# Sums of silu(h) formed in the output stage, conversions spread anew, and each output sum issued behind its product

## The chip, the cores and the metric

The kernel runs on one core of a Trainium2 chip. The metric is device time in microseconds (us), the median of some runs. A core has a matrix engine (TensorE, PE in the profile), a vector engine (VectorE, DVE), a scalar engine (ScalarE, ACT) and GpSimd (POOL), each with a queue of its own that is worked off in order; DMAs are issued mostly from SyncE's queue (SP). Matmuls read operands from SBUF, the on-chip memory, and add into PSUM, the accumulator memory of eight banks; DVE and ACT read the results there.

## The reference, cut to what matters

```python
def reference(q, k, v, moe_w1, moe_w2, moe_w3, moe_w_out, moe2_w_in, moe2_w_out):
    attn = window_attention(q, k, v)            # 4 x 8 heads x 576 x 64, window of 64
    x = attn.transpose(0, 2, 1, 3).reshape(2304, 512)
    x = ((x @ w1) * (x @ w2)) @ w3 @ w_out      # 512 -> 1024 -> 1024 -> 512
    h = x @ w_in                                # 512 -> 2048
    g = h * (1.0 / (1.0 + np.exp(-h)))          # silu
    return (g @ w_out2).astype(np.float32)      # 2048 -> 512, 2304 tokens
```

The weights arrive as 64-bit floats and are made into 32-bit ones on the chip ("conversion").

## The kernel before, in words

**Arithmetic.** Every product of two 32-bit matrices is three matmul passes: each operand is split into a rounded part (hi, a cast on ACT) and a rest (lo, a subtraction on DVE), and hi·hi, hi·lo and lo·hi are added up in PSUM (`PASSES`). On top of this the last two layers use a Strassen scheme: a 2x2 product of blocks costs seven products k = 0..6 (named A11, A12, A22, S1 to S4 after the left operand) and sums of the operands before and of the results behind.

**Stages.** The attention and the first feed-forward run block by block (`phase_a`, six blocks). During the sixth, `hooks5(n)` interleaves the first preparation for the next layer: slot n counts from 0 to 23 (n5 + n = −24 to −1 in `jobs`). Then comes the **h stage**: 12 pieces of work d (a duo: 256 hidden units by 768 tokens) of seven slots each, `h_slot(d, pos)`, in the order `POS` of the products. A product is 12 matmuls of 128x384. `read` takes its result out of PSUM (ACT or DVE) and applies silu. Then the **output stage**: 36 sets m, nine groups of 256 tokens (`tg`) by four parts of the hidden units (e = m % 4); `out_products(m)` is 7 products of 6 matmuls 128x256, added up over e in two PSUM tiles a and b of two banks each (`AT` says where). After the fourth set of a group `out_sums(tg)` puts the seven results together (one on ACT, then `two`, `u3`, `u4` and the two halves of c on DVE) and stores the group.

**Between the two stages** silu(h) goes through device memory (`gd`). In before `sums_of_g(d - 1, pos)` makes the Strassen sums S1 to S4 of a duo's four blocks while the next duo is computed, two operations of 128x768 on DVE and two on POOL, and `keep` stores seven pieces of 384 KB per duo. The output stage loads seven pieces of a set (`f_load`, two DMAs), casts them (`f_high`: 128x256 and 128x1536 on ACT) and subtracts (`f_low`: the same shapes on DVE), three sets ahead of the products.

**What sets the order.** The source is the order: each engine works off its instructions in the order of the calls below, and waits on semaphores for what it needs. `jobs` is a table from slot to calls: `at(slot, f, ...)`. `convert(n, at, places)` puts the steps of one conversion of w_out2 (loads, ACT L220 and L225, DVE L228 and L232, POOL L237, then sums and stores to `t32`) into slots at−2 to at+7; `PLAN` and the list in `hooks5` say where the eight conversions start. `w_part` (table `W5` for n = 0..3) makes the split operands of w_in out of what `r_load` loads; `o_load` and `o_part` do it for w_out2; `x_raw`, `x_sum`, `x_op` for the tokens. Line L800 is the helper `tt` through which every elementwise sum or difference goes, so its rows are told apart by their tiles: gq, gxb, gxa and gst are the buffers of the h stage, f and xe loaded sets, hi, lo and a their split parts, ot and oc the output sums, ab and a (L707, L709) the first feed-forward's activations.

Of the kernel before, what the change touches and what calls it, by code (L numbers as in the profile page):

```python
# [9 lines left out]
F32 = mybir.dt.float32  # L10
# [12 lines left out]
NB = 384  # L23
# [19 lines left out]
def tile_window_attention_ffn(ctx, tc, qkv, qkp, vp, w1, w2, w3t, w_out, w_in, w_out2, out):  # L43
# [704 lines left out]
    with tc.manual_schedule():  # L748
# [44 lines left out]
        gd = dram.tile([NTG, DUOS, 128, 7, 256], F32, name="gd", tag="gd")  # L793
# [82 lines left out]
        def convert(n, at, places):  # L876
# [5 lines left out]
            (l0, s0, r0, f0, h0, i0, _), (l1, s1, r1, f1, h1, i1, _) = [c.pieces() for c in pair]  # L882
# [23 lines left out]
            for k, f in ((-2, l0), (-1, l1), (0, s0), (0, r0), (1, f0), (1, s1), (2, h0), (2, i0), (2, r1)):  # L906
                jobs.setdefault(at + k, []).append(f)
            for k, f in ((3, f1), (3, h1), (4, i1), (5, sums), (6, more), (6, store_b), (7, store_t)):
                jobs.setdefault(at + k, []).append(f)
# [11 lines left out]
        def o_load(n):  # L921
            t = raw["o", n] = [xe[:, 0:1024], xe[:, 1024:1792]] if n in (1, 3, 5) else [st[2], st[3][:, 0:768]]
            for x, y in zip(t, (slice(0, 4), slice(4, 7))):
                nc.sync.dma_start(out=x, in_=t32[n, :, y].rearrange("p a n -> p (a n)"))

        def o_tiles(n):
# [8 lines left out]
            t = pair_tiles("wo", n - 1, (2, 256))  # L935
            oop[n] = [(x[:, 0], x[:, 1]) for x in t]

        def o_part(n, part):
            if part == 0:
                o_tiles(n)  # L940
            r0, r1 = raw["o", n]
            src = [r0[:, 0:512], r0[:, 512:1024], r1[:, 0:512], r1[:, 512:768]]
# [74 lines left out]
        S2, S3, S1, A22, A12, S4, A11 = range(7)  # L1017

        def read(d, k):
# [9 lines left out]
            elif k == 2:  # L1029
                silu(g["a11", d % 2], h_bank("ha"))  # L1030
            elif k == 3:
                add(nc.vector, one, h_bank("hb"), one)
                add(nc.vector, h_bank("hc"), h_bank("hc"), one)
                silu(g["a12", d % 2], h_bank("hc"))
# [47 lines left out]
        def f_load(m):  # L1082
            if m >= NTG * DUOS:
                return
            if m == 0:
                t = slot("f0", "x0", [6, 256], pool=end), xe[:, 2048:2304]
            elif m == 1 or m % 3 == 0:
                t = xe[:, 0:1536].rearrange("p (a n) -> p a n", a=6), xe[:, 1536:1792]
            elif m == 2 or m % 3 == 1:
                q = slot(f"f{m}", "q", [7, 256])  # L1090
                t = q[:, 0:6], q[:, 6]
            else:
                t = slot(f"f{m}", "xa", [6, 256]), slot(f"fa{m}", "xb", [256])
            raw["f", m] = t
            tg, e = divmod(m, DUOS)
            nc.sync.dma_start(out=t[0], in_=gd[tg, e, :, 0:6])
            nc.sync.dma_start(out=t[1], in_=gd[tg, e, :, 6])

        def f_high(m):
            if m < NTG * DUOS:  # L1100
                n = m % 4
                if n == 3:
                    lo = shared["wo", "p"].rearrange("p a n -> p (a n)")[:, 0:1536].rearrange("p (a n) -> p a n", a=6)
                    a = unit_tile("wo", 6, 3)[:, 512:1024]
# [8 lines left out]
                nc.scalar.copy(out=a[0], in_=raw["f", m][1])  # L1113
                nc.scalar.copy(out=hi, in_=raw["f", m][0])  # L1114

        def f_low(m):
            if m < NTG * DUOS:
                lo, hi, a = sets[m]
                f, fa = raw["f", m]
                sub(nc.vector, a[1], fa, f32(a[0]))  # L1120
                sub(nc.vector, lo, f, f32(hi))

        TERMS = ((A11, 0, 0), (S2, 2, 1), (S3, 0, 1), (S1, 2, 0), (A22, 3, 0), (A12, 1, 0), (S4, 1, 1))
# [3 lines left out]
        def out_products(m):  # L1129
# [5 lines left out]
            for (op, w, half), (x, y, z), first in zip(TERMS, AT, FIRST):  # L1135
                dst = bank[x][:, y, z * 256 : z * 256 + 256]
                for q in range(2):
                    cols = slice(q * 128, q * 128 + 128)
                    lhs = [x[:, cols] for x in a] if op == A11 else [hi[:, op, cols], lo[:, op, cols]]
                    rhs = [x[:, half] for x in oop[2 * e + q][w]]  # L1140
                    for n, (l, r) in enumerate(PASSES):
# [3 lines left out]
                        )  # L1145

        def out_sums(tg):
# [5 lines left out]
            t = slot(f"ot{tg}", "st", [4, 256], bufs=4)  # L1153
            one, u4, two, u3 = [t[:, i] for i in range(4)]
            c = slot(f"oc{tg}", "st", [2, 2, 256], bufs=4)
            nc.scalar.copy(out=one, in_=b[:, 1, 0:256])
            add(nc.vector, two, a[:, 1, 0:256], one)
            add(nc.vector, u3, a[:, 1, 256:512], two)
            add(nc.vector, u4, a[:, 0, 256:512], two)
            halves = [x.rearrange("p (i n) -> p i n", i=2) for x in (a[:, 0], b[:, 0])]  # L1160
            add(nc.vector, c[:, 1], halves[0], t[:, 3:4].to_broadcast([128, 2, 256]))
            j, r = divmod(tg, 3)
            row = j * 2 * NB + r * 128
            nc.sync.dma_start(out=out[row + NB : row + NB + 128, :], in_=c[:, 1].rearrange("p i n -> p (i n)"))
            if tg < NTG - 1:
# [193 lines left out]
```

## Time and profile before

| | |
|---|---|
| three runs | 884.75, 885.05 and 887.29 us, median 885.05 |
| the profiled execution's own time | 887.39 us |
| its span in the trace | 884.9 us |
| PE busy | 827.5 us (94%) |
| DVE, ACT, POOL busy | 650.8, 539.4, 408.2 us |
| end of the sixth block and start of the h stage | 481.6 us |
| start of the output stage's transition | 678.4 us |
| end of the last matmul | 878.9 us |

A row of the table by stretches gives, for each engine, busy time and (x) the number of instructions in a stretch, then the clock that was granted to PE (1.00 is 2.4 GHz, 0.50 is 1.2 GHz), the busy share of the DMA engines and GB/s. A row of the waits gives what an engine stood still for: instruction <- releaser, the sum, how many times, the longest. A row of the timeline gives start, duration, engine, line, what is written and read, and in brackets how long the engine stood idle before it and what ended that. In a grouped row the second number is the mean in ns.

### The profile page before, as it was taken

To read this page: it belongs to the slowest core of one execution; us is meant where nothing else is said; L and a number is where in the kernel's file an instruction comes from. 1 tells how busy PE (TensorE), PEld (TensorE's weight loads), DVE (VectorE), ACT (ScalarE), POOL (GpSimd) and SP (SyncE) were. 2 spreads that over 40 slices of the span, in tenths; PEclk is the share of its full clock that TensorE was granted. 3 is DMA by queue.
4 is the path that set the end of the run, shared out by engine and by line. 5 is a ranking of instruction groups with operands and counts; after the bars stand their busy time and mean duration, and the time that the engine had idled before them with its cause. 6 is when DMAs were issued, how large, how long until landed. Compare 5 with 4: busy or idle time off the path is not lost. (4 is left out here: it accounts for less than half of the span.)

```text
span 884.9 us, 15592 instructions
## 1 busy us (share of the span) xinstructions
PE 827.5 (94%) x5066; PEld 777.4 (88%) x5066; DVE 650.8 (74%) x1419; ACT 539.4 (61%) x1254; POOL 408.2 (46%) x460
## 2 busy tenths in 40 slices
PE   8899999999999999999859999879997969999997
PEld 3455899999999999999859999779897969999997
DVE  8879777788888888883794789968878655545551
ACT  7889778898888998984543345424455344343330
POOL 5767666677676776774672353564232000000000
PEclk9999999999999999999998999998999979999999
DMA  9997235345445445434524567897888687565631
GB/s 309 342 295 236 76 99 164 102 136 183 149 141 172 135 157 168 150 117 143 206 80 149 166 223 254 278 348 242 270 290 303 219 322 264 196 222 198 222 128 38
DMA packets 96689, 174.66 MB, mean 197 GB/s; under 512 B 8160, under 2 KB 64864, under 8 KB 96608
## 3 DMA queue, kind: packets, MB, share of 16 engines
q1 hardware_dynamic: 93008, 168.82, 57.1%
q10 hardware_dynamic: 3600, 4.85, 1.5%
q8 instruction: 40, 0.66, 0.3%
q14 instruction: 41, 0.34, 0.1%
HBM read 119.64 MB, written 54.00 MB: 196 GB/s over the span
## 5 line engine op out<-in xcount | busy, mean ns | idle before, releaser
L693 PE MATMUL ab<-xa,hl 128*128 128x384 f32 x576 | 121.3, 345 | 9.2 <-DVE a L709 6.2
L693 PE MATMUL ab<-xb,hl 128*128 128x384 f32 x570 | 116.7, 337 | 0.0
L693 PEld LDWEIGHTS ab<-xa,hl 128*128 128x128 f32 x576 | 100.3, 191 | 10.7 <-DVE a L709 7.2
L693 PEld LDWEIGHTS ab<-xb,hl 128*128 128x128 f32 x570 | 101.9, 191 | 0.0
L1142 PE MATMUL oa<-wo_w,hi 128*128 128x256 f32 x486 | 89.8, 283 | 0.0
L1142 PEld LDWEIGHTS oa<-wo_w,hi 128*128 128x128 f32 x486 | 75.7, 191 | 0.0
L351 POOL TENSOR_TENSOR klo<-qk,qkhi 64x192 fp32r<-64x192 f32 x110 | 67.3, 612 | 8.4 <-ACT qkhi L345 2.3
L723 PE MATMUL x<-p,wp 128*128 128x384 f32 x360 | 70.4, 344 | 0.0
L474 POOL TENSOR_TENSOR xr<-ot 128x128 f32<-128x128 f32 x55 | 32.7, 595 | 72.9 <-DVE ot L473 56.0
L723 PEld LDWEIGHTS x<-p,wp 128*128 128x128 f32 x360 | 63.3, 192 | 0.0
L237 POOL TENSOR_TENSOR cv_b<-cv_b,cv_r 128x512 int32<-128x512 int32 x32 | 48.6, 1518 | 18.7 <-DVE cv_b L232 10.6
L1114 ACT CAST hi<-f 128x1536 fp32r<-128x1536 f32 x24 | 35.4, 1475 | 35.1 <-PE ob L1142 35.1
L999 PE MATMUL hb<-xop,wi_w 128*128 128x384 f32 x252 | 50.6, 349 | 5.4 <-DVE gxb L800 5.4
L999 PE MATMUL ha<-xop,wi_w 128*128 128x384 f32 x252 | 49.8, 345 | 6.3 <-ACT gq L1008 5.7
L800 DVE TENSOR_TENSOR lo<-f,hi 128x1536 fp32r<-128x1536 f32 x18 | 31.7, 1758 | 30.5 <-ACT hi L1114 30.4
L999 PEld LDWEIGHTS hb<-xop,wi_w 128*128 128x128 f32 x252 | 46.7, 196 | 6.3 <-DVE gxb L800 6.3
L999 PEld LDWEIGHTS ha<-xop,wi_w 128*128 128x128 f32 x252 | 45.1, 191 | 7.5 <-ACT gq L1008 6.1
L999 PE MATMUL hd<-xop,wi_w 128*128 128x384 f32 x252 | 49.1, 341 | 2.3 <-DVE gxb L800 2.2
L1142 PE MATMUL oa<-wo_w,lo 128*128 128x256 f32 x180 | 51.0, 283 | 0.0
L406 ACT ACTIVATE sm<-sm,nm 128x192 f32<-128x192 f32 x110 | 49.3, 449 | 1.4
L999 PEld LDWEIGHTS hd<-xop,wi_w 128*128 128x128 f32 x252 | 44.2, 188 | 4.2 <-DVE gxb L800 3.3
L345 ACT CAST qkhi<-qk 128x768 fp32r<-128x768 f32 x55 | 46.0, 836 | 1.2
(245 smaller groups left out, 2297.5 us busy)
## 6 DMA issues: line engine op xcount, KB each, us to landing
qk<-in_qkv SPq DMA_DIRECT2D x55, 384.0 KB, 3.0
f<-gd SPq DMA_DIRECT2D x24, 768.0 KB, 4.3
gd<-gq SPq DMA_DIRECT2D x24, 384.0 KB, 3.6
gd<-gxb SPq DMA_DIRECT2D x24, 384.0 KB, 3.1
gd<-gst SPq DMA_DIRECT2D x24, 384.0 KB, 2.9
xe<-gd SPq DMA_DIRECT2D x12, 768.0 KB, 4.3
words<-in_w3t SPq DMA_DIRECT2D x16, 512.0 KB, 6.4
words<-in_w SPq DMA_DIRECT2D x16, 512.0 KB, 7.0
```

The lines of the kernel that those rows point to most:

```text
L237: nc.gpsimd.tensor_tensor(out=self.b, in0=self.b, in1=self.r, op=ALU.add)
L345: nc.scalar.copy(out=hi, in_=t)
L351: nc.gpsimd.tensor_tensor(out=k_lo[g % 2][hs, h * 192 : h * 192 + 192], in0=t[hs, n], in1=f32(hi[hs, n]), op=ALU.subtract)
L406: nc.scalar.activation(out=e[:, h, :], in_=x, func=AF.Exp, scale=-1.0, bias=nm[:, h : h + 1], accum_out=sums_of[g % 2][:, h, 0:1])
L474: nc.gpsimd.tensor_tensor(out=xr[:, c, r : r + 128], in0=t[:, 0:128], in1=t[:, 128:256], op=ALU.add)
L693: nc.tensor.matmul(acc, lhsT=w[:, l, fs], rhs=x[k // 2][:, k % 2, r, :], start=(k == 0 and n == 0), stop=(k == 3 and n == 2),)
L723: nc.tensor.matmul(acc, lhsT=wp[f][:, l, o * 128 : (o + 1) * 128], rhs=p[f][:, r, :], start=(f == 0 and n == 0), stop=(f == 7 and n == 2),)
L800: eng.tensor_tensor(out=out, in0=a, in1=b, op=op)
L999: nc.tensor.matmul(bank[name][:, q, 0:NB], lhsT=w[:, l, first + kt], rhs=x[:, kt, r, :], start=(fresh and kt == 0 and n == 0), stop=(kt == ...
L1114: nc.scalar.copy(out=hi, in_=raw["f", m][0])
L1142: nc.tensor.matmul(dst, lhsT=lhs[l], rhs=rhs[r], start=(first and e == 0 and q == 0 and n == 0), stop=(e == DUOS - 1 and q == 1 and n == 2 ...
```

## The change

Five things are changed together.

1. `sums_of_g` is gone. `gd` holds four pieces per duo (A11, A12, A22 and A21), `keep` is called four times, and the sums S1 to S4 are made per set in the output stage, by the new `f_sums(m)`: S1 on POOL (on DVE for sets 0 to 3), S3, S2 and S4 on DVE, 128x256 each. `f_load` is one DMA of 512 KB. Casts and subtractions of a set are 768 + 768 + 256 wide.
2. The buffers of the h stage have new homes: the q buffer is now free during it and takes the loads of the conversions and of some weights; a11 and a12 have one buffer, and nothing is summed in place of a22.
3. The conversions are spread anew: two in the sixth block (at slots 2 and 6), six in the h stage (at 12, 18, 25, 31, 37, 43) instead of three and five; their sign step is one DVE instruction of 512 instead of two of 256.
4. Loads and preparations have new slots (`W5`, `r_load`, `o_load`, `f_load`).
5. `out_sums(tg, op)` is called behind each of the seven products of a group's last set, each time for one sum, instead of once after the set. In the last group the last 128x512 sum is two halves, as before, the first of them behind A12.

```diff
-        S2, S3, S1, A22, A12, S4, A11 = range(7)
...
-                silu(g["a11", d % 2], h_bank("ha"))
+                silu(g["a11"], h_bank("ha"))
...
-        def sums_of_g(d, pos):
-            a11, a12, a22, a21, s2 = g["a11", d % 2], g["a12", d % 2], g["a22"], g["two", d % 2], g["s2"]
-            if pos == 0:
-                keep(d, A12, a12)
-                keep(d, A22, a22)
-            elif pos == 3:
-                add(nc.vector, a22, a21, a22)
-                sub(nc.vector, s2, a22, a11)
-                sub(nc.gpsimd, a11, a21, a11)
-            elif pos == 4:
-                sub(nc.gpsimd, a12, a12, s2)
-                keep(d, S1, a22)
-                keep(d, S2, s2)
-            elif pos == 5:
-                keep(d, S3, a11)
-            elif pos == 6:
-                keep(d, S4, a12)
...
             run_later()
-            if d:
-                sums_of_g(d - 1, pos)
-            if pos == 4:
-                keep(d, A11, g["a11", d % 2])
             run_jobs(7 * d + pos)
+            if pos == 0 and d:
+                keep(d - 1, 1, g["a12"])
+                keep(d - 1, 2, g["a22"])
+            elif pos == 4:
+                keep(d, 0, g["a11"])
+                if d:
+                    keep(d - 1, 3, g["two", 1 - d % 2])
...
+        def f_sums(m, eng=None):
+            if m < NTG * DUOS:
+                f, t = [x.rearrange("p (a n) -> p a n", a=4) for x in raw["f", m]]
+                add(eng or nc.gpsimd, t[:, 0], f[:, 3], f[:, 2])
+                sub(nc.vector, t[:, 1], f[:, 3], f[:, 0])
+                sub(nc.vector, t[:, 2], t[:, 0], f[:, 0])
+                sub(nc.vector, t[:, 3], f[:, 1], t[:, 2])
...
+                if e == DUOS - 1:
+                    out_sums(tg, op)
...
-        W5 = {0: 8, 1: 10, 2: 16, 3: 17}
+        W5 = {0: 8, 1: 15, 2: 17, 3: 19}
...
-                for i, (first, x) in enumerate(((2, 2), (5, 0), (9, 2))):
+                for i, (first, x) in enumerate(((2, 2), (6, 0))):
...
-        PLAN = ((3, 24), (4, 29), (5, 34), (6, 39), (7, 44))
+        PLAN = ((2, 12), (3, 18), (4, 25), (5, 31), (6, 37), (7, 43))
...
         out_products(0)
+        keep(NDUO - 1, 1, g["a12"])
+        keep(NDUO - 1, 2, g["a22"])
+        f_sums(2, nc.vector)
         f_high(2)
         f_low(2)
+        f_load(3)
         product(NDUO - 1, 6)
+        read(NDUO - 1, 6)
+        keep(NDUO - 1, 3, g["two", 1 - NDUO % 2])
         for part in range(4):
             o_part(7, part)
+        f_sums(3, nc.vector)
         f_high(3)
         f_low(3)
-        read(NDUO - 1, 6)
-        for pos in (0, 3, 4, 5, 6):
-            sums_of_g(NDUO - 1, pos)
-        for m in (4, 5, 6):
-            f_load(m)
+        f_load(4)
+        f_load(5)
+        f_load(6)
+        f_sums(4)
         for m in range(1, NTG * DUOS):
+            f_sums(m + 4)
             f_high(m + 3)
             f_low(m + 3)
             f_load(m + 6)
             out_products(m)
-            if m % DUOS == DUOS - 1:
-                out_sums(m // DUOS)
```

The first place is PE's row in the last set of the second group (m = 7). A row is line, operation, out<-in with buffer numbers, the shape, how many alike follow each other, and in brackets the engines whose semaphores it waits for. oa1 and ob1 are the group's PSUM tiles. Before, from the end of the second product (S2) on:

```order
L1142 MATMUL oa1_8152<-wo_w23_7945,wo_p_7946 128x256
L1142 MATMUL oa1_8152<-wo_w17_7795,hi7_8144 128x256 x2
L1142 MATMUL oa1_8152<-wo_w17_7795,wo_p_7946 128x256
L1142 MATMUL oa1_8152<-wo_w21_7943,hi7_8144 128x256 x2
L1142 MATMUL oa1_8152<-wo_w21_7943,wo_p_7946 128x256
L1142 MATMUL oa1_8152<-wo_w19_7797,hi7_8144 128x256 x2
L1142 MATMUL oa1_8152<-wo_w19_7797,wo_p_7946 128x256
L1142 MATMUL oa1_8152<-wo_w23_7945,hi7_8144 128x256 x2
L1142 MATMUL oa1_8152<-wo_w23_7945,wo_p_7946 128x256
L1142 MATMUL oa1_8152<-wo_w20_7774,hi7_8144 128x256 x2
L1142 MATMUL oa1_8152<-wo_w20_7774,wo_p_7946 128x256
L1142 MATMUL oa1_8152<-wo_p_7946,hi7_8144 128x256 x2
```

and with the change, from the same point on:

```order
L1150 MATMUL oa1_8097<-wo_p_7875,lo7_8086 128x256
L1150 MATMUL oa1_8097<-wo_w17_7712,hi7_8087 128x256 [waits DVE_49]
L1150 MATMUL oa1_8097<-wo_w17_7712,hi7_8087 128x256
L1150 MATMUL oa1_8097<-wo_w17_7712,lo7_8086 128x256
L1150 MATMUL oa1_8097<-wo_p_7875,hi7_8087 128x256 x2
L1150 MATMUL oa1_8097<-wo_p_7875,lo7_8086 128x256
L1150 MATMUL oa1_8097<-wo_w19_7714,hi7_8087 128x256 [waits DVE_49]
L1150 MATMUL oa1_8097<-wo_w19_7714,hi7_8087 128x256
L1150 MATMUL oa1_8097<-wo_w19_7714,lo7_8086 128x256
L1150 MATMUL oa1_8097<-wo_p_7875,hi7_8087 128x256 x2
L1150 MATMUL oa1_8097<-wo_p_7875,lo7_8086 128x256
L1150 MATMUL oa1_8097<-wo_w20_7694,hi7_8087 128x256 [waits DVE_49]
```

The matmuls are the same; with the change the first matmul of the third product (S3), of the fourth (S1) and of the fifth (A22) waits for a DVE instruction, which before none within the set did.

The second place is DVE's row at the end of the same group (lo, wo_p and a11 are the rests of later sets, gq and xe the loaded sets, fs the sums of one, ot and oc the output sums). Before:

```order
L800 TENSOR_TENSOR a11_7821<-f10_8149,a11_7821 128x256 [waits DMAHW2_49,PE_49,Activation_49]
L800 TENSOR_TENSOR lo10_8298<-f10_8149,hi10_8299 128x1536 [waits DMAHW1_49,PE_49,Activation_49]
L800 TENSOR_TENSOR ot1_8349<-oa1_8152,ot1_8349 128x256 [waits Activation_49]
L800 TENSOR_TENSOR ot1_8349<-oa1_8152,ot1_8349 128x256 [waits DVE_49]
L800 TENSOR_TENSOR ot1_8349<-oa1_8152,ot1_8349 128x256
L800 TENSOR_TENSOR oc1_8350<-oa1_8152,ot1_8349 128x512 [waits DVE_49]
L800 TENSOR_TENSOR oc1_8350<-ob1_8153,ot1_8349 128x512 [waits DVE_49,PE_49]
```

and with the change:

```order
L800 TENSOR_TENSOR gq_6173<-gq_6173 128x256 [waits DMAHW4_49]
L800 TENSOR_TENSOR gq_6173<-gq_6173 128x256 [waits Pool_49]
L800 TENSOR_TENSOR gq_6173<-gq_6173 128x256 [waits DVE_49]
L800 TENSOR_TENSOR lo10_8255<-f10_8094,hi10_8256 128x768 [waits PE_49,Activation_49]
L800 TENSOR_TENSOR lo10_8255<-fs10_8095,hi10_8256 128x768 [waits Activation_49]
L800 TENSOR_TENSOR a11_7738<-fs10_8095,a11_7738 128x256 [waits PE_49,Activation_49]
L800 TENSOR_TENSOR ot1_8272<-oa1_8097,ot1_8272 128x256 [waits PE_49,Activation_49]
L800 TENSOR_TENSOR ot1_8272<-oa1_8097,ot1_8272 128x256 [waits DVE_49,PE_49]
L800 TENSOR_TENSOR ot1_8272<-oa1_8097,ot1_8272 128x256 [waits PE_49]
L800 TENSOR_TENSOR oc1_8273<-oa1_8097,ot1_8272 128x512 [waits DVE_49,PE_49]
L800 TENSOR_TENSOR oc1_8273<-ob1_8098,ot1_8272 128x512 [waits DVE_49,PE_49]
```

The three ot sums stand behind the subtractions of set 10 as before, and now also behind the sums of set 11; what waits for PE in them is now each one by itself.

The third place is POOL's row in the h stage, about the fourth conversion (cv_b, cv_u: the conversion's buffers). Before:

```order
L237 TENSOR_TENSOR cv_b_6879<-cv_b_6879,cv_r_6881 128x512 [waits DMAHW4_49,DVE_49,Activation_49]
L800 TENSOR_TENSOR gq_6210<-gq_6210 128x768 [waits DMAHW1_49,DMAHW5_49,DVE_49,Activation_49]
L237 TENSOR_TENSOR cv_b_6904<-cv_b_6904,cv_r_6925 128x512 [waits DMAHW5_49,DVE_49]
L800 TENSOR_TENSOR gq_6210<-gq_6210,gst1_6214 128x768 [waits DMAHW6_49]
L800 TENSOR_TENSOR cv_b_6879<-cv_b_6879,cv_b_6904 128x256 [waits DVE_49,Pool_49]
L800 TENSOR_TENSOR cv_u_6981<-cv_b_6904,cv_t_6980 128x256 [waits DMAHW3_49,DVE_49]
```

and with the change, about the conversions that take its place:

```order
L887 TENSOR_TENSOR cv_b_6672<-cv_b_6672,cv_r_6674 128x512 [waits DMAHW5_49,DVE_49,Activation_49]
L887 TENSOR_TENSOR cv_b_6698<-cv_b_6698,cv_r_6720 128x512 [waits DMAHW0_49,DVE_49,Activation_49]
L800 TENSOR_TENSOR cv_b_6672<-cv_b_6672,cv_b_6698 128x256 [waits DVE_49,Pool_49]
L800 TENSOR_TENSOR cv_u_6775<-cv_b_6698,cv_t_6774 128x256 [waits DMAHW1_49,DVE_49]
L887 TENSOR_TENSOR cv_b_6798<-cv_b_6798,cv_r_6800 128x512 [waits DMAHW6_49,DVE_49,Activation_49]
L887 TENSOR_TENSOR cv_b_6819<-cv_b_6819,cv_r_6840 128x512 [waits DMAHW0_49,DMAHW4_49,DVE_49,Activation_49]
```

The sums of silu(h), 128x768 on gq, gxa and gst0, are gone from between the conversions' steps.

## Rows read from the trace of the kernel before

**Rows 1.** Table by stretches: sixth block, h stage, transition, output stage; then h stage's last part.

```profile
410.00:481.60 71.60, 57.31 (x293) 55.18 (x292) 49.26 (x65) 30.32 (x58) 38.50 (x33) 0.90 0.48 164
481.60:678.40 196.80, 182.84 (x997) 178.60 (x995) 154.91 (x182) 87.53 (x135) 78.44 (x54) 0.97 0.77 258
678.40:720.30 41.90, 27.91 (x193) 26.75 (x193) 24.19 (x29) 15.43 (x21) 5.70 (x3) 0.83 0.72 248
720.30:878.90 158.60, 158.56 (x1334) 158.36 (x1332) 82.20 (x101) 55.66 (x69) 0.00 (x0) 0.99 0.57 195
640.00:678.40 38.40, 38.40 (x216) 37.66 (x214) 30.09 (x36) 20.37 (x35) 10.72 (x6) 1.00 0.89 307
```

**Rows 2.** Waits of PE from 405 us to the end, the longest groups.

```profile
PE ob L1142 <- ACT a L1113: 7.2, 1, 7.2
PE ab L693 <- DVE a L709: 6.2, 2, 4.6
PE ha L999 <- ACT gq L1008: 5.7, 1, 5.7
PE hb L999 <- DVE gxb L800: 5.4, 2, 4.1
PE ob L1142 <- DVE gxb L800: 3.5, 1, 3.5
PE x L723 <- ACT q L114: 3.2, 1, 3.2
PE ab L693 <- ACT a L707: 2.9, 1, 2.9
PE x L723 <- POOL q L117: 1.9, 1, 1.9
```

**Rows 3.** Timeline of ACT before the wait of 5.7 us, in the h stage.

```profile
596.52 0.67 ACT L220 ACTIVATE cv_b<-gst 128x512 f32<-128x512 f32 x1 [9.30 <-DMA gst<-in_w_out]
```

**Rows 4.** Groups of instructions of the h stage, shapes apart.

```profile
L800 POOL TENSOR_TENSOR gq<-gq,gst 128x768 f32<-128x768 f32 x6 | 12.6, 2107 | 0.0
L800 DVE TENSOR_TENSOR gst<-gxb,gq 128x768 f32<-128x768 f32 x6 | 5.7, 958 | 0.4
L237 POOL TENSOR_TENSOR cv_b<-cv_b,cv_r 128x512 int32<-128x512 int32 x10 | 13.8, 1382 | 16.7 <-DVE cv_b L232 8.6 <-issue 3.7 <-ACT cv_b L220 1.6
```

**Rows 5.** Timeline of the transition: POOL, SP's queue, ACT.

```profile
708.02 1.82 POOL L800 TENSOR_TENSOR gst<-gst,gst 128x768 f32<-128x768 f32 x1
...
710.32 0.44 SPq L1096 DMA_DIRECT2D f<-gd  x1
...
715.68 0.40 ACT L1113 CAST a<-f 128x256 fp32r<-128x256 f32 x1 [11.65 <-DMA f<-gd]
```

**Rows 6.** Timeline of ACT at a set's start in the output stage.

```profile
774.77 1.48 ACT L1114 CAST hi<-xe 128x1536 fp32r<-128x1536 f32 x1 [3.16 <-PE ob L1142]
```

**Rows 7.** Timeline of DVE about the end of the same group.

```profile
776.28 1.76 DVE L800 TENSOR_TENSOR lo<-xe,hi 128x1536 fp32r<-128x1536 f32 x1 [2.85 <-ACT hi L1114]
780.28 1.22 DVE L800 TENSOR_TENSOR ot<-oa,ot 128x256 f32<-128x256 f32 x3 [2.24 <-ACT ot L1156]
```

**Rows 8.** Chain that ended last, its end: start, duration, what.

```profile
869.66 2.82 PE oa L1142 x24
872.48 2.12 PE ob L1142 x18
...
877.45 1.43 PE ob L1142 x12
...
881.45 0.33 DVE oc L800
```

**Rows 9.** Table by stretches: the clock behind waits of 1.6, 4.6 and 1.2 us.

```profile
444.40:446.00 1.60, 1.60 (x9) 1.60 (x10) 1.60 (x1) 1.60 (x4) 1.60 (x2) 1.00 0.00 0
453.70:456.00 2.30, 2.30 (x7) 2.30 (x8) 2.30 (x2) 2.30 (x5) 2.30 (x2) 0.50 0.17 57
...
634.70:636.00 1.30, 1.27 (x7) 1.28 (x8) 1.29 (x2) 0.17 (x1) 0.00 (x0) 1.00 1.10 277
```

More of the change, by code (lines that the diff above doesn't have):

```diff
@@ L881, in convert, with rest @@
             pair = [Stored(None, w_out2[f * 128 : (f + 1) * 128, :], places[f % 2]) for f in (2 * n, 2 * n + 1)]
-            (l0, s0, r0, f0, h0, i0, _), (l1, s1, r1, f1, h1, i1, _) = [c.pieces() for c in pair]
+            def rest(c):
+                nc.vector.scalar_tensor_tensor(
+                    out=c.b, in0=c.high, scalar=-0x80000000, in1=c.b, op0=ALU.bitwise_and, op1=ALU.bitwise_or
+                )
+                nc.gpsimd.tensor_tensor(out=c.b, in0=c.b, in1=c.r, op=ALU.add)
+            (l0, s0, r0, f0, _, _, _), (l1, s1, r1, f1, _, _, _) = [c.pieces() for c in pair]
+            i0, i1 = [lambda c=c: rest(c) for c in pair]
             t = {}
@@ L1112, in f_high @@
                 sets[m] = lo, hi, a
[L1113 to L1114 removed]
+                f, t = raw["f", m]
+                for i, x in ((0, f), (3, t)):
+                    nc.scalar.copy(out=hi[:, i : i + 3], in_=x[:, 0:768].rearrange("p (a n) -> p a n", a=3))
+                nc.scalar.copy(out=a[0], in_=t[:, 768:1024])
         def f_low(m):
@@ L1118, in f_low @@
                 lo, hi, a = sets[m]
-                f, fa = raw["f", m]
-                sub(nc.vector, a[1], fa, f32(a[0]))
-                sub(nc.vector, lo, f, f32(hi))
+                f, t = raw["f", m]
+                for i, x in ((0, f), (3, t)):
+                    sub(nc.vector, lo[:, i : i + 3], x[:, 0:768].rearrange("p (a n) -> p a n", a=3), f32(hi[:, i : i + 3]))
+                sub(nc.vector, a[1], t[:, 768:1024], f32(a[0]))
+        A11, A12, A22, S1, S3, S2, S4 = range(7)
         TERMS = ((A11, 0, 0), (S2, 2, 1), (S3, 0, 1), (S1, 2, 0), (A22, 3, 0), (A12, 1, 0), (S4, 1, 1))
@@ L1145, in out_products, with out_sums @@
                         )
[L1147 removed]
+                if e == DUOS - 1:
+                    out_sums(tg, op)
+        def out_sums(tg, op):
             a, b = bank["a"], bank["b"]
[L1153 removed]
+            if op == A11:
+                tmp["t"] = slot(f"ot{tg}", "st", [4, 256], bufs=4)
+                tmp["c"] = slot(f"oc{tg}", "st", [2, 2, 256], bufs=4)
+            t, c = tmp["t"], tmp["c"]
             one, u4, two, u3 = [t[:, i] for i in range(4)]
[L1155 to L1161, printed above, removed]
             j, r = divmod(tg, 3)
             row = j * 2 * NB + r * 128
[L1164 to L1170 removed]
+            if op == A11:
+                nc.scalar.copy(out=one, in_=b[:, 1, 0:256])
+            elif op == S2:
+                add(nc.vector, two, a[:, 1, 0:256], one)
+            elif op == S3:
+                add(nc.vector, u3, a[:, 1, 256:512], two)
+            elif op == S1:
+                add(nc.vector, u4, a[:, 0, 256:512], two)
+            elif op == A22:
+                x = a[:, 0].rearrange("p (i n) -> p i n", i=2)
+                add(nc.vector, c[:, 1], x, t[:, 3:4].to_broadcast([128, 2, 256]))
+                nc.sync.dma_start(out=out[row + NB : row + NB + 128, :], in_=c[:, 1].rearrange("p i n -> p (i n)"))
+            elif tg == NTG - 1:
+                i = 1 if op == S4 else 0
+                add(nc.vector, c[:, 0, i], b[:, 0, i * 256 : i * 256 + 256], t[:, i])
                 (nc.sync if i else nc.scalar).dma_start(
```

101 lines of the change are left out of this document (53 added, 48 removed).

## The prediction

> **What bounds the kernel now.** I read the table by stretches first [rows 1]. The kernel is bound by PE, but not evenly. In the output stage PE is busy for 158.56 of 158.6 us, and a set costs 2.82 + 2.12 = 4.94 us [rows 8], 0.71 us for each of its seven products. The h stage runs at 38.40 us for 216 recorded matmuls in its undisturbed part, 0.178 us each, so that a product of 12 takes 2.13 us; its 83 products are worth 177 us and take 196.8. The sixth block has 288 matmuls of the same shape, 51 us, and takes 71.6. From 678.4 to 878.88 [rows 8] are 200.5 us, and the last of the 84 products and 36 sets are worth 180.0; all of that loss lies in the transition, where PE is busy for 27.9 of 41.9 us, some of it at half clock. So about 20 us are lost in each of three stretches and none in the fourth.
>
> The waits of PE say to whom [rows 2]: in the sixth block DVE's a (6.2 us in two waits), ACT's q and a (3.2, 2.9) and POOL's q (1.9), 14.2 together; in the h stage 5.7 for ACT and 5.4 for DVE; in the transition 7.2 for ACT and 3.5 for DVE. The rest of each loss is the clock. Behind the wait of 4.6 us PE ran at 0.50, behind those of 1.6 and 1.2 us at 1.00 [rows 9]: a long wait is paid a second time with 1.5 to 2.5 us, a short one isn't.
>
> **The change part by part.** The sums are set against the profiled execution's 887.39 us, which lies 2.34 us above the median of the three runs; that is taken off at the end. Some 0.3%, 2.7 us, is what a measurement of this kernel can tell from no change.
>
> Sixth block: a third conversion leaves it, with its two L237, L228 and four L232 steps and its loads, and the weight parts for n = 1 to 3 come 5, 1 and 2 slots later. The two waits for DVE's a (6.2) have such steps ahead of them in DVE's queue and should go, with the half clock behind the longer (2.0); the waits for q (5.1, and some 2 of half clock) stand behind POOL and ACT work that thins out, and I count half of those 7. The 2.9 for ACT, behind a conversion's load, stays. That makes −8.2 − 3.5, say −12, between −8 and −14.
>
> h stage: per duo two DVE operations of 0.96 us and two POOL operations of about 2.1 [rows 4] go, and three stores of 384 KB; on POOL they are what stretches and delays the conversions' steps. Against that one more conversion comes: two L237 of 1.38 on POOL and its steps on DVE and ACT. All of it lies beside PE. What stood on the path are the DVE waits (5.4, and some short ones) and the ACT wait of 5.7, in which ACT stood 9.30 us before a conversion's load [rows 3]; that load was queued on SP behind token loads, and has its own buffer and an earlier slot now. With the half clock behind two of them the stage lost 19.8. I leave 3.8 of that, a short wait at each of the two token loads with a conversion beside it: −16, between −11 and −19.
>
> Transition: before, ACT waited 11.65 us for the load of set 4, which SP issued at 710.32, behind the store of S4 that came out of two POOL sums (the last ends at 709.84) [rows 5]. Now no sum stands there, and the load goes out behind the last product's silu alone. But `two` of the first group stands in DVE's queue behind the subtractions of set 6, and so S3 of set 3 waits until sets 4 to 6 are loaded, cast and subtracted. Each is some 3.8 us on DVE (1.76 + 0.41 [rows 7] and up to four sums of 0.41), behind a load that stands in line. I get, as an estimate, a stall there of 10.7 us in place of the 7.2 in set 4, and one of 2.2 at the stage's first set in place of 3.5 and what follows it. With 1.3 for the first group's S1 and A22 (below) and 2.7 for the clock, 16.9 of the 20.5 stay lost: −3.6, between −7 and +2.
>
> Groups: this is the price of the change. The order shows waits for DVE before S3, S1 and A22 of each group's last set, where none was. The S3 wait is for `two`, behind the subtractions of the set three ahead. Their hi buffers are free when A12 of the set before is done, 0.71 us before the set's start T. The first cast of 768 takes about 0.8 (half of 1.48 [rows 6], and a little), the two subtractions of 768 1.8 (1.76 as one [rows 7]), the small one 0.35: T − 0.7 + 0.8 + 1.8 + 0.4 = T + 2.3. `two` is 0.41 (three in 1.22 [rows 7]) and ends at T + 2.7; S3 could have started at T + 1.41. That is 1.4 us, up to 2.0 if the sums of the set four ahead get between. S1 and A22 wait from the end of the product ahead to the end of one sum, 0.41 + some 0.26 for the two hand-overs = 0.67 each. A group costs 3.05 us; the seven between the first and the last 21.4. The last group has nothing in DVE's queue and pays 4 x 0.67 = 2.7. Together +24, between +19 and +30.
>
> The Trainium skill (PSUM — Partial Sum Buffer, section "PSUM bank collisions raise a hardware error") speaks against summing between the products: it wants PSUM guarded by bank, not by address, since no two engines may be in one bank at once. S2 and S3 share a bank, and so do S1 and A22, but not S3 and S1; by the page alone the S1 wait need not be, and the groups would cost 0.67 x 8 = 5.4 less, the sum coming to 875; the order shows that wait, and no row of before has an output sum beside a product.
>
> Clock: the three waits of a group add up to 3 us within less than 5, with two products between. Before shows single waits of up to 1.9 us at full clock and from 2.9 on at half; it shows no such cluster. So I let three of the eight groups fall to half clock, at 1.7 each: +5, between 0 and +20.
>
> Other work in the output stage: DVE gets the sums, three or four of 0.35 to 0.41 per set, onto 2.2 us of subtractions, with the output sums under 4.4 us of 4.94; it fits. POOL's one sum is beside. Loads shrink from 768 to 512 KB. I count nothing for these.
>
> Tail: before, PE ends at 878.88, the last sum at 881.78 [rows 8], the span at 884.9, 3.1 later. Now only one 128x256 sum is behind the last product, 0.45. That is 3.57 instead of 6.02: −2.5.
>
> Sum: −12 − 16 − 3.6 − 2.5 + 24 + 5 = −5.1, so 882.3 for an execution like the profiled one, and 880 against the median.
>
> **The rivals.**
> *The clock falls in every group* (slower). If the three waits of a group count together, PE is at half clock behind each of the eight, and at 1.7 us that is 13.6 instead of 5: 888.6; at 2.5 us, 895. I take 891. It decides between a wait of 1.9 us, which left the clock, and one of 2.9, which did not [rows 2]; a group's 3.05 lies past that, but in pieces. The first group's stall is long and halves it in any case.
> The Trainium skill (TensorE: Matmul & The Clock Gate, section "HAM oscillation — how this bites in real kernels") tells of a loop whose every step waits so long that every next step starts cold, and of another with frequent short pauses that does so too. By it this rival would be the rule; the trace of before, with its short waits at full clock, doesn't bear that out for pauses this small.
> *The early gains stay out by half in the h stage* (same). Six conversions in it, each with 1.38 us steps on POOL beside DVE's work, keep the DVE waits at half, 3.8, and one half clock of 1.7: +5.5 over the forecast, 885.5. For it: the waits follow whichever instruction is late, and the conversions stay. Against: POOL loses 24 operations of 2.1 us and DVE 24 of 0.96.
> *The groups are cheap* (faster). If DVE and ACT are further ahead than I think and `two` comes at once, a group pays 3 x 0.67 = 2 us, the groups 16 + 2.7 with the clock untouched, 18 to 19 in place of 29: about 869. For it: DVE stood idle for half of the output stage before. Against: the buffers that set 10's subtraction needs come free only 0.71 us before T.
>
> **How the numbers follow.** The forecast, 880 with its own bounds 872 to 887, has 0.47; the clock in every group 0.20; the early gains by half 0.15; the cheap groups 0.18. Faster (under 882.4): 0.38 of the forecast's 0.47, the cheap groups, 0.04 of the third: 0.60. Within 0.3%: 0.06 + 0.09 + 0.02 = 0.17. Slower (over 887.7): 0.18 + 0.03 + 0.02 = 0.23. The range reaches from the cheap groups with better early gains (864) to the clock in every group (893).
>
> **What would show it.** In the changed kernel's trace the h stage should start near 470 us instead of 481.6 and take some 181 us; waits of PE for ot should stand in each group's last set, one of 1.4 to 2.0 and two of 0.67, with the granted clock at 0.5 behind some; the first group should stall at S3; and the last matmul should be 3.6 us before the end. I am wrong if the h stage keeps waits of over 3 us, if the ot waits are under 0.7 or over 2.5, or if the first group's stall is below 5 or beyond 15 us.

## The result, and the profile after

The change made the kernel slower: 891.13 us (median of four runs, 890.85 to 891.3) against 885.71 for the kernel before beside it, a ratio of 1.0059 with an interval of 1.0042 to 1.0077: little, but clear of noise. The forecast was 880, faster; the time lies within the stated range (864 to 893) and on the wrong side of no change. The profiled execution's span is 888.3 us, against 884.9.

Where the time went is read by the ends of the stages, in the table by stretches of the changed kernel (columns as in [rows 1]: busy time and instructions of PE, PEld, DVE, ACT, POOL, then granted clock, DMA share, GB/s):

```profile
410.00:471.80 61.80, 53.49 (x292) 51.47 (x291) 41.52 (x52) 27.98 (x53) 34.43 (x29) 0.97 0.42 149
471.80:648.90 177.10, 176.78 (x998) 175.58 (x996) 121.17 (x163) 91.75 (x143) 39.53 (x36) 1.00 0.77 238
648.90:685.80 36.90, 21.35 (x150) 20.96 (x151) 34.00 (x59) 16.16 (x27) 4.79 (x5) 0.81 0.53 165
685.80:885.20 199.40, 178.62 (x1374) 172.45 (x1374) 121.46 (x215) 56.65 (x95) 23.67 (x27) 0.94 0.26 93
```

| | before | after | difference | forecast |
|---|---|---|---|---|
| start of the h stage | 481.6 | 471.8 | −9.8 | −12 |
| h stage | 196.8 | 177.1 | −19.7 | −16 |
| from its end to the last matmul | 200.5 | 236.3 | +35.8 | −3.6 + 24 + 5 = +25.4 |
| from there to the end of the span | 6.0 | 3.1 | −2.9 | −2.5 |

So the first 650 us are 29.5 us better, about as forecast. The h stage is the clearest: its 83 products take 177.1 us, which is their own pace (177), and the granted clock is 1.00 throughout. The output stage gives back more than all of it. PE's waits from 640 us on say to whom (instruction <- releaser: us in total, times, longest):

```profile
PE oa L1150 <- DVE ot L800: 32.4, 27, 12.1
PE ob L1150 <- DVE lo L800: 2.8, 1, 2.8
PE ob L1150 <- DVE gxb L800: 0.6, 1, 0.6
PE ob L1150 <- DVE oc L800: 0.5, 1, 0.5
```

27 of them are for ot, the sums `two`, `u3` and `u4`, three in each of nine groups, and none is in [rows 2]. They stand where the order put them. This is PE's timeline at one of the two costliest of the later groups (start, duration, line, what, and in brackets the idle time before and its releaser):

```profile
758.91 0.50 PE L1150 MATMUL oa<-wo_w,hi 128*128 128x256 f32 x2 [1.77 <-DVE ot L800]
...
760.40 0.58 PE L1150 MATMUL oa<-wo_w,hi 128*128 128x256 f32 x2 [0.52 <-DVE ot L800]
...
762.35 0.80 PE L1150 MATMUL oa<-wo_w,hi 128*128 128x256 f32 x2 [0.52 <-DVE ot L800]
```

and DVE's before the first of them:

```profile
755.83 2.36 DVE L800 TENSOR_TENSOR lo<-xe,hi 128x768 fp32r<-128x768 f32 x2 [1.64 <-ACT hi L1119]
758.11 0.41 DVE L800 TENSOR_TENSOR a<-xe,a 128x256 fp32r<-128x256 f32 x1
758.45 0.41 DVE L800 TENSOR_TENSOR ot<-oa,ot 128x256 f32<-128x256 f32 x1
```

`two` stands behind the subtractions of the set three ahead, which begin when ACT's cast is done; the operand of `two`, the product S2, is done at 757.1. The seven waits before S3 in groups 2 to 8 are 1.24 to 1.77 us, those before S1 and A22 0.52 each. In the first group the same order costs far more (PE, then DVE):

```profile
685.80 0.80 PE L1150 MATMUL oa<-wo_w,hi 128*128 128x256 f32 x2 [12.15 <-DVE ot L800]
```
```profile
675.81 0.94 DVE L800 TENSOR_TENSOR lo<-f,hi 128x768 fp32r<-128x768 f32 x1
...
677.88 1.21 DVE L800 TENSOR_TENSOR xe<-xe 128x256 f32<-128x256 f32 x3
679.00 1.82 DVE L800 TENSOR_TENSOR lo<-gq,hi 128x768 fp32r<-128x768 f32 x2
...
682.73 2.35 DVE L800 TENSOR_TENSOR lo<-xe,hi 128x768 fp32r<-128x768 f32 x2
685.00 0.41 DVE L800 TENSOR_TENSOR a<-xe,a 128x256 fp32r<-128x256 f32 x1
685.34 0.41 DVE L800 TENSOR_TENSOR ot<-oa,ot 128x256 f32<-128x256 f32 x1
```

DVE works without a pause on sets 4, 5 and 6 and on the sums of set 7, and PE stands until it comes to the one small sum that set 3's third product waits for. On SP's queue the loads of sets 4 and 5 (at 665.82 and 666.35 us) stand behind the store of the h stage's last piece (665.37); that of set 6 went out at 671.03, when set 3's first subtraction had read the buffer.

The end of the chain of waits of the changed kernel shows a wait's whole price (start, duration, what):

```profile
879.05 0.99 PE oa L1150 x6
880.04 0.02 issue
880.07 0.44 DVE ot L800
880.50 0.04 issue
880.54 0.98 PE oa L1150 x6
...
885.23 0.42 DVE oc L800
```

From the start of one product to that of the next are 1.49 us instead of the 0.71 of [rows 8]: 0.52 idle, and 0.27 because six matmuls that start and end alone take 0.98 to 0.99, with the clock at full. The tail is as meant: one sum of 0.42 behind the last matmul.

### The profile page after: what moved, and what is told of

Its sections match the earlier page's. It is cut to its first block, busy times and chain, and to the rows that moved or that the text cites. A ratio compares the mean times of both kernels' runs of the same rounds, so it can differ in the third digit from the quotient of the medians.

```text
span 888.3 us, 15643 instructions
## 1 busy us (share of the span) xinstructions
PE 831.2 (94%) x5066; PEld 779.0 (88%) x5066; DVE 656.5 (74%) x1527; ACT 542.5 (61%) x1290; POOL 388.1 (44%) x468
## 5 line engine op out<-in xcount | busy, mean ns | idle before, releaser
L1150 PE MATMUL oa<-wo_w,hi 128*128 128x256 f32 x432 | 85.5, 293 | 32.4 <-DVE ot L800 32.4
L1150 PEld LDWEIGHTS oa<-wo_w,hi 128*128 128x128 f32 x432 | 67.8, 194 | 38.4 <-DVE ot L800 38.4
L800 POOL TENSOR_TENSOR fs<-f 128x256 f32<-128x256 f32 x11 | 10.2, 928 | 153.0 <-DMA f<-gd 141.0
L1150 PE MATMUL oa<-wo_w,lo 128*128 128x256 f32 x216 | 61.9, 286 | 0.0
L1016 PE MATMUL hb<-xop,wi_w 128*128 128x384 f32 x252 | 48.4, 339 | 0.0
L1119 ACT CAST hi<-gq 128x768 fp32r<-128x768 f32 x26 | 20.5, 832 | 44.3 <-issue 42.9
L392 DVE CUSTOM_DVE_ANT_0 sm<-s,consts 128x192 f32<-128x192 f32 x144 | 45.2, 351 | 1.3 <-PE s L385 0.9
L1016 PEld LDWEIGHTS hb<-xop,wi_w 128*128 128x128 f32 x252 | 44.7, 188 | 0.0
```

The source lines that it names most:

```text
L392: nc.vector.tensor_tensor_reduce(out=sm[g % 2][:, h, :], in0=s_ps[:, h, :], in1=consts[:, at + 64 - 64 * h : at + 256 - 64 * h], op0=ALU.a ...
L800: eng.tensor_tensor(out=out, in0=a, in1=b, op=op)
L1016: nc.tensor.matmul(bank[name][:, q, 0:NB], lhsT=w[:, l, first + kt], rhs=x[:, kt, r, :], start=(fresh and kt == 0 and n == 0), stop=(kt == ...
L1119: nc.scalar.copy(out=hi[:, i : i + 3], in_=x[:, 0:768].rearrange("p (a n) -> p a n", a=3))
L1150: nc.tensor.matmul(dst, lhsT=lhs[l], rhs=rhs[r], start=(first and e == 0 and q == 0 and n == 0), stop=(e == DUOS - 1 and q == 1 and n == 2 ...
```

## The experiments

Two theories for the output stage. **Theory 1**: the place of the sums makes the loss, since PE waits for them in the middle of a set; the sums behind the set would cost nothing. **Theory 2**: with the sums of silu(h) DVE is short of time there, and the waits for ot only show it; it would appear as waits for lo or a elsewhere.

### All sums after the set

```diff
-                if e == DUOS - 1:
-                    out_sums(tg, op)
+            if e == DUOS - 1:
+                for op, _, _ in TERMS:
+                    out_sums(tg, op)
```

> The changed kernel with part 5 alone undone: all sums of a group are issued after the last set's seven products, as in before; everything else as changed. Theory 1 (the place of the sums makes the loss): in the changed kernel's trace the waits for ot cost 21 us in groups 2 to 8 (1.24 to 1.77 before S3, 0.52 each before S1 and A22, and some 0.165 of refilling the pipe each time), the first group 12.15 + 1.04 and 5 of half clock behind, two later groups 6.8 of half clock, the last group 2.8. All that goes, the tail gets 2.9 longer: 891 - 21 - 18.5 - 6.8 - 2.8 + 2.9 = 845, no wait of PE for ot. Theory 2 (DVE is short of time at the start of the output stage, and the sums' place only decides where PE feels it): the stall of 12 us moves to the start of set 4, 5 or 6, waiting for lo or a, and 857 to 865 is measured.

Measured 845.28 us, 0.957 of before (0.954 to 0.960). Its output stage in the table by stretches:

```profile
649.40:686.00 36.60, 32.69 (x250) 32.10 (x251) 33.66 (x58) 18.70 (x31) 4.65 (x5) 0.95 0.51 162
686.00:836.40 150.40, 150.40 (x1276) 150.21 (x1274) 120.81 (x213) 54.28 (x90) 27.47 (x27) 1.00 0.34 123
```

No wait for ot is left among PE's waits from 640 us on, PE is busy for 150.40 of 150.40 us from 686 on, and DVE does the same work there, 120.81 us, as in the changed kernel over a longer time (121.46). More telling is DVE at the first group, where theory 2 wanted the stall to move:

```profile
679.89 1.82 DVE L800 TENSOR_TENSOR lo<-gq,hi 128x768 fp32r<-128x768 f32 x2
...
683.63 2.37 DVE L800 TENSOR_TENSOR lo<-xe,hi 128x768 fp32r<-128x768 f32 x2
685.93 0.41 DVE L800 TENSOR_TENSOR a<-xe,a 128x256 fp32r<-128x256 f32 x1
686.26 1.20 DVE L800 TENSOR_TENSOR ot<-oa,ot 128x256 f32<-128x256 f32 x3
```

The subtractions of sets 5 and 6 run within a microsecond of where they ran before, and PE, which goes on with set 4, is held up for 0.39 us in all. DVE was full but in time; only the sum's place in its queue made PE wait. Theory 2 falls.

### The sums ahead of the next sets' work, still behind their products

```diff
         for m in range(1, NTG * DUOS):
+            if m % DUOS == DUOS - 1:
+                out_products(m)
             f_sums(m + 4)
...
-            out_products(m)
+            if m % DUOS < DUOS - 1:
+                out_products(m)
```

> The changed kernel, but in a group's last set the products with their sums are issued ahead of the next sets' sums, casts and subtractions, so that on DVE the group's sums stand before them; the sums stay behind their products. Theory 1: the waits before S3 shrink from 1.24 to 1.77 to the 0.52 of the other two, the first group's 12.15 to 0.52; the three waits of 0.52 in each of nine groups stay (some 18 us with refilling): about 864, with the clock no longer falling in the groups. Theory 2: the subtractions that are now later make PE wait for lo or a at a later set; the first group's stall is found at set 4 to 6, and 872 or more is measured.

Measured 876.66 us. That is a time that theory 2 asked for (872 or more), but its sign is missing: from 640 us on PE waits for ot, and the only wait for lo or a is the one of 2.8 at the first set, as in the changed kernel.

```profile
PE oa L1150 <- DVE ot L800: 23.2, 27, 9.2
PE ob L1150 <- DVE lo L800: 2.8, 1, 2.8
```

In the later groups theory 1's numbers came: 0.59 before S3 and 0.52 before S1 and A22 in every one, with the clock at full. The first group's wait is 9.20 instead of 0.52, though: moving its sums ahead of set 6's and 7's work left sets 4 and 5 in front, as the source issues those before set 3's products. I had counted only the one set that I moved past. That wait and the clock behind it (half until 9.8 us after its end) are the 13 us by which the expectation was missed.

### The sums that read a behind A22, the last product into a

```diff
-                if e == DUOS - 1:
-                    out_sums(tg, op)
+                if e == DUOS - 1 and op in (A11, A22, S4):
+                    for x in {A11: (A11,), A22: (S2, S3, S1, A22), S4: (A12, S4)}[op]:
+                        out_sums(tg, x)
```

> The changed kernel, but the sums that read the PSUM tile a (two, u3, u4 and one half of c) are issued together behind A22, the last product into a, and the rest behind S4, the last into b; one stays behind A11. PE then writes b while DVE reads a. Theory 1: no wait of PE in a group's last set, the tail nearly as short as in the changed kernel: 842, some 3 us below the kernel with all sums after the set. Theory 2: as there, a stall of some 12 us at set 4 to 6: 855 or more.

Measured 850.16 us, 8 more than expected. There is no wait for ot from DVE, but one of 4.2 us in the first group for ACT, whose timeline shows it:

```profile
681.75 0.83 ACT L1119 CAST hi<-xe 128x768 fp32r<-128x768 f32 x1 [1.23 <-DVE xe L800]
682.49 0.40 ACT L1120 CAST a<-xe 128x256 fp32r<-128x256 f32 x1
682.80 0.36 ACT L1172 COPY ot<-ob 128x256 f32<-128x256 f32 x1
```

`one` is still issued behind A11, reads tile b, and stands in ACT's queue behind the casts of set 6; A12, which writes b, waits for it. It is the same mechanism on another engine. The rest of the difference is half clock behind that wait and in the sixth block: the h stage starts at 474.6 us, 2.9 later than in the kernel with all sums after the set. The edit does not reach that block. In the traces of the six kernels that share its code the h stage starts between 471.0 and 474.6, so that these 2.9 us lie within the spread between executions; the one profiled here, of 852.06 us, is the slowest of four.

### Only the first sum behind its product

```diff
-                if e == DUOS - 1:
-                    out_sums(tg, op)
+                if e == DUOS - 1 and op in (A11, S2, A22, S4):
+                    for x in {A11: (A11,), S2: (S2,), A22: (S3, S1, A22), S4: (A12, S4)}[op]:
+                        out_sums(tg, x)
```

> The changed kernel, but behind S2 only the first sum (two) is issued; u3, u4 and half of c go behind A22 and the rest behind S4. So the waits before S3 stay as they are (12.15 in the first group, 1.24 to 1.77 in the others) and those before S1 and A22 go: 9 groups x 2 x 0.69 = 12 us. For the clock: if the short waits of 0.52 are what keeps it at half behind the long one (it stays at 0.50 from 678.8 to 695.9 with two of them in it), the half clock behind the stall ends 3 to 7 us sooner and the two later groups at half clock stay at full: 12 + 2.5 + 6.8 less, about 870. If the long wait alone sets it: 877 to 879.

Measured 872.01 us, 19 less than the changed kernel and near the 870 of the first case. The waits before S3 are all there (12.44 in the first group, 1.24 to 1.77 later, 0.59 in the last), those before S1 and A22 are gone. One of the two later groups still fell to half clock. For the clock, the table by stretches behind the first group's wait, of the changed kernel (wait until 685.8) and of this one (until 689.0):

```profile
685.80:695.90 10.10, 9.07 (x39) 8.48 (x40) 3.02 (x7) 1.87 (x3) 0.72 (x1) 0.50 0.12 48
695.90:700.00 4.10, 4.10 (x37) 4.10 (x37) 3.47 (x7) 0.74 (x2) 0.00 (x0) 1.00 0.54 192
```
```profile
689.00:695.30 6.30, 6.24 (x29) 6.24 (x30) 1.36 (x4) 0.88 (x2) 0.73 (x1) 0.50 0.09 34
695.30:700.00 4.70, 4.70 (x42) 4.70 (x42) 4.28 (x9) 1.16 (x3) 0.00 (x0) 1.00 0.43 146
```

Behind a wait of 12 us PE stays at half clock for 10.1 us where two waits of 0.52 follow, and for 6.3 us where none does. The kernel with the sums ahead (9.8 behind a wait of 9.2, with two) and that with sums behind A22 (5.9 behind one of 4.2, with none) fit. The last section says why this is not enough to show the short waits as the cause.

### The kernel before with this part alone

```diff
-            if m % DUOS == DUOS - 1:
-                out_sums(m // DUOS)
...
+                if e == DUOS - 1:
+                    out_sums(tg, op)
```

> The kernel before with part 5 alone: each output sum is issued behind its product, nothing else is changed. Theory 1: the same waits as in the changed kernel appear before S3, S1 and A22: some 21 us in groups 2 to 8 and 2.8 in the last, 2.9 gained at the tail. In the first group S3 of set 3 waits for the subtractions of set 6, whose load goes out behind set 4's: before, those were done at about 724 while S3 could have started at 706, and the stall of 7.2 at set 4 is swallowed: +12 to +18 with half clock behind. Together 885 + 33 to 40 and 3 to 7 for the clock: about 922. Theory 2 (the waits came with the new loads and sums on DVE): under 900.

Measured 930.13 us, 1.051 of before (1.048 to 1.055), 8 more than expected. PE's waits for ot:

```profile
PE oa L1142 <- DVE ot L800: 44.6, 27, 19.7
```

19.7 us of it are in the first group, where 12 to 18 with half clock behind were expected. The waits need nothing of the new loads and sums. They are a little longer here, 2.15 before S3: cast and subtraction are not split, and in DVE's timeline the subtraction of 1.76 us starts only when ACT's cast of 1.48 is through.

### The kernel before without the sums of silu(h)

```diff
-            elif pos == 3:
-                add(nc.vector, a22, a21, a22)
-                sub(nc.vector, s2, a22, a11)
-                sub(nc.gpsimd, a11, a21, a11)
             elif pos == 4:
-                sub(nc.gpsimd, a12, a12, s2)
                 keep(d, S1, a22)
-                keep(d, S2, s2)
+                keep(d, S2, a21)
```

> The kernel before, with the four sums of silu(h) per duo left out (two 128x768 on DVE, two on POOL); seven pieces are stored as before, unsummed, so this leaves out a part of the computation. If these sums are what held up the h stage: its waits for DVE gxb (5.4 and 2.3) and the half clock behind one of them go, the wait of 5.7 for ACT behind a conversion's load stays: h stage 185 to 188 instead of 196.9; at set 4 the load goes out some 4 us sooner: 884 - 10 - 5 = 869. If the spread of the conversions and loads did it: h stage within 3 us of before, 879 or more.

Measured 865.89 us, 0.979 of before (0.976 to 0.981). The h stage:

```profile
481.70:664.80 183.10, 179.30 (x999) 178.65 (x997) 116.44 (x164) 89.14 (x137) 34.69 (x32) 0.98 0.84 281
```

It takes 183.1 us instead of 196.8: 13.7 of the 19.7 us belong to the sums. Two waits remain, both for ACT (2.8 and 1.0), the first the one behind a conversion's load of [rows 3]; they and the clock are the other 6. What of the change removed those is not shown by this kernel; the next one bears on it.

### The conversions where they were

```diff
-                for i, (first, x) in enumerate(((2, 2), (6, 0))):
+                for i, (first, x) in enumerate(((2, 2), (5, 0), (9, 2))):
...
-        PLAN = ((2, 12), (3, 18), (4, 25), (5, 31), (6, 37), (7, 43))
+        PLAN = ((3, 24), (4, 29), (5, 34), (6, 39), (7, 44))
```

> The kernel with all sums after the set (845.3), but with the conversions in the slots of before: three in the sixth block (2, 5, 9), five in the h stage (24, 29, 34, 39, 44). It tells what part 3 gives in the sixth block: if the third conversion held it up, the waits for DVE's a grow back from 2.5 to some 6 us with half clock behind, and the h stage starts 5 to 9 us later, 850 to 854. If the later weight parts (part 4) did it, the h stage starts within 2 us and 844 to 847 is measured; the h stage with one conversion less has no wait of PE to lose.

Measured 849.77 us. The two stages:

```profile
410.00:477.50 67.50, 57.22 (x292) 55.69 (x290) 47.65 (x58) 29.92 (x56) 39.85 (x33) 0.90 0.48 166
477.50:653.60 176.10, 176.10 (x997) 175.79 (x996) 113.20 (x157) 89.50 (x139) 34.82 (x32) 1.00 0.73 228
```

The h stage starts 5.8 us later than in the kernel with the sums after the set (471.7), and is 1.6 shorter. Measured against all six kernels with the new slots (471.0 to 474.6) the start is 2.9 to 6.5 us later. So the third conversion's move is worth some 3 to 6 of the 10 us in the sixth block, and costs 1.6 in the h stage; the rest is left for the later weight parts and loads, which were not tried by themselves. In the h stage PE waits for nothing, although the conversions stand where they stood before. The wait behind a conversion's load, 5.7 in [rows 2] and 2.8 without the sums, therefore did not need the new slots; which of the other parts removed it is open.

### What the findings make together

```diff
+                if tg < NTG - 1:
+                    ready = {S4: (A11, S2, S3, S1, A22, A12, S4)}
+                else:
+                    ready = {A11: (A11,), A22: (S2, S3, S1, A22), S4: (A12, S4)}
                 if e == DUOS - 1:
-                    out_sums(tg, op)
+                    for x in ready.get(op, ()):
+                        out_sums(tg, x)
...
+        at(FIRST_OUT + 22, f_load, 0)
+        at(FIRST_OUT + 26, f_low, 0)
         for n, first in ((0, 2), (1, 10), (2, 12), (3, 16), (4, 18), (5, 23), (6, 24)):
...
-        at(FIRST_OUT + 22, f_load, 0)
...
-        at(FIRST_OUT + 26, f_low, 0)
```

> The changed kernel with the sums after the set, in the last group behind A22 (a) and behind S4 (b), and with the subtractions of set 0 ahead of the preparation of w_out2 in the slot they share. Against the kernel with all sums after the set (845.3): the tail ends some 4.3 us behind the last matmul instead of 6.0, the wait of 2.8 for lo at the first set becomes 1.3 and the half clock behind it (3.4 long) goes: 845.3 - 1.7 - 1.5 - 1.7 = 840. If DVE only puts the wait elsewhere (gxb, or lo of set 1): 843 to 845.

Measured 840.8 us, 0.951 of before (0.949 to 0.953): faster than both kernels. In its chain of waits the last group has no break between its products. The sums of a start at 832.24, beside A12 and S4, which PE works on from 831.97 to 833.55; the span ends 4.3 us behind the last matmul, as expected:

```profile
829.28 2.87 PE oa L1150 x24
...
832.24 0.43 DVE ot L800
...
833.46 0.60 DVE oc L800
834.06 0.33 DVEq L1384
834.39 0.33 DVE oc L800
```

The wait for lo at the first set shrank from 2.8 to 0.55, but two others, of 1.68 and 0.43, came up at 669 us, also for lo. The clock stayed at full through the h stage and the output stage up to the last matmul.

## Why the prediction was wrong

**Right: what bounds the kernel, and the early gains.** Some 20 us were lost in each of three stretches; the sixth block and the h stage gave 29.5 of them, 28 were forecast. In the sixth block the waits for a shrank from 6.2 to 3.4 and did not go, which is about the 2 us missing there (and less than the spread of that stage between executions, 3.6); in the h stage the loss went entirely where I left 3.8. That the sums on POOL and DVE were the larger part of it is shown by the kernel without the sums; that the new slots of the conversions were not needed for the smaller part, by the kernel with the old ones.

**Right: the groups.** The order's waits came at the three places, and with the sizes: 1.24 to 1.77 against 1.4 to 2.0, and 0.52 idle with 0.27 for ending and starting against 0.67. Summed, seven groups at 1.48 + 2 x 0.52 + 3 x 0.27 and a last one of 3.2 make 26.5; 24 was forecast. The clock fell in two of those groups:

```profile
760.70:767.50 6.80, 6.28 (x30) 5.99 (x29) 2.02 (x4) 1.87 (x3) 0.63 (x1) 0.50 0.10 39
832.40:839.20 6.80, 5.77 (x26) 5.39 (x26) 1.54 (x3) 1.24 (x2) 0.72 (x1) 0.50 0.10 39
```

Half of 6.28 and of 5.77 busy us are some 6 us of PE's time lost, 3 for each, where 5 was forecast for three at 1.7.

**Wrong: the transition.** Of the loss of 56 us in the output stage (236.3 less the 180 of its matmuls) 26.5 and 6 are the groups and their clock; some 24 are left for the transition, and 16.9 were forecast, between 13.5 and 22.5. The stall at set 3's S3 was 12.15 instead of 10.7, the first set's wait 3.4 (0.6 and 2.8) instead of 2.2. The larger part is the clock: 2.7 were set for it. PE was at half for 10.1 us behind the stall, busy for 9.07 of them, as shown above, and about the first set's wait:

```profile
651.50:658.30 6.80, 5.52 (x26) 5.52 (x27) 6.07 (x12) 2.11 (x4) 0.00 (x0) 0.50 0.60 188
```

Half of 9.07 and of 5.52 are 4.5 and 2.8, some 7 us. The step that failed is that term, "with 2.7 for the clock": I took the price of one long wait from before, and the transition had two. The first set's wait, for which I set nothing beyond its own length, cost 2.8 in the clock; the stall cost 4.5 instead of 2.7. S1 and A22 wait twice right behind the stall, but that these waits made it dearer is not shown. Against the forecast the transition cost 7 us more, the groups 3.5 (2.5 in waits, 1 in the clock) and the sixth block 2; the h stage and the tail gave 4 beyond theirs. Together these turn −5.1 into the +3.4 of the span.

Two readings behind the terms were wrong as well. The forecast says that before shows no cluster of waits, and a wait of 1.9 us that left the clock at full. But the 1.9 of [rows 2] (for POOL's q, until 462.98) and the 3.2 for ACT's q (463.43 to 466.61) lie 0.45 us apart, and the clock fell at 463.85, within the second: that is a cluster, and it fell. A wait of 1.9 us at full clock stands elsewhere in that trace, at 24.8 us, for DVE's sm. And a set's load before was 896 KB in its two DMAs (768 and 128), not 768; nothing was counted for it.

**The rivals.** The time is the one that I worked out for the clock falling in every group, 891, but that isn't what happened: five of seven groups stayed at full clock, and the early gains were all there. A time that fits a rival doesn't show it; the granted clock by stretches does. The second loop that the forecast takes from the Trainium skill, the one with frequent short pauses, stands there in the page's next section (TensorE: Matmul & The Clock Gate, section "A second HAM failure mode: psum-queue depth-cycling"). The traces do not agree with it for pauses this small: with waits of 0.52 to 0.59 alone, eight groups of the kernel with the sums ahead stayed at full. The cheap groups did not come, since `two` is not free before set m + 3's subtractions. That the early gains stay out by half is refuted by the h stage's 177.1.

What the forecast did not weigh is the change's best use: the groups' waits in the order come from part 5 alone, which cost some 45 us in the runs, and nothing else of the change needs it. The Trainium skill's rule on PSUM banks (PSUM — Partial Sum Buffer, section "PSUM bank collisions raise a hardware error") spoke against just that part. The wait before S1, which the rule by bank would not ask for, is there in the trace at 0.52 like the others; no run here took that one away alone.

## What to carry to other kernels

When a small consumer of a matmul's result is put between matmuls that write the same accumulator tile, and the program makes them wait for each other as here, the matrix engine waits for it, and for everything that stands ahead of it in the consumer's queue; find its place in that queue before its own duration. Issue such consumers where the matrix engine goes on in another tile, and shorten a tail only where the tail is. A change with five parts should be costed part by part also for leaving one out: here four of them were worth 39 us, and the fifth cost 46.

## What the runs showed of the hardware that was not expected

The same cluster of waits did not always have the same effect on the clock. In the kernel before with the sums behind their products, seven groups waited 2.15, 0.52 and 0.52 us alike; the clock fell in one (around 752) and stayed at full in the others, as here in the next:

```profile
752.00:756.00 4.00, 3.48 (x17) 3.40 (x17) 1.11 (x2) 0.00 (x0) 0.00 (x0) 0.50 0.16 61
...
773.50:780.00 6.50, 3.32 (x23) 2.91 (x24) 3.30 (x5) 0.54 (x2) 0.00 (x0) 1.00 0.53 187
```

In the changed kernel it fell in the two groups whose first wait was 1.77 us and in none of the five with less; with that wait alone, in the kernel with only `two` behind its product, it fell at one of two.

The same is seen where not even the program differs. Six kernels (the changed one and those with all sums after the set, with the sums ahead, behind A22, with `two` alone, and the combined one) share the code of the sixth block. In it each has a wait of 1.94 to 1.97 us for DVE's a, about 449 us into the span. The clock fell within 1.6 us behind it in three of them and stayed at full in the other three. So the length of a wait does not decide alone, and what else does was not taken apart here.

Nor is the length of a stay at half clock the same each time. About the wait of 2.8 us at the first set it was 6.8 us long in three kernels (the changed one, behind A22, `two` alone) and 3.4 in three others (all sums after the set, the sums ahead, the old slots), with the same code there. This bears on the waits of 0.52 us that follow a long one. With two of them the clock stayed at half for 10.1 and 9.8 us behind the long wait, and for 8.0 in the kernel before with the sums behind their products; without them it was 6.3 and 5.9. The order fits, but the differences are of the size of the 3.4 us by which equal cases differ, so it is not shown that the short waits prolong the stay.
